# Softmax attention beside linear attention on one core: GpSimd's pattern copies as 64-bit integer additions with the addend in the instruction

## The chip, the cores and the metric

The kernel runs on one core of one Trainium2 chip. The metric is the device time of one execution in microseconds (us). It is given as the median of the runs; for the kernel before, two runs gave 650.61 and 651.38 us, with a median of 651.0 us.

## The reference, cut to what matters

Two independent attention blocks, A (linear) and B (softmax), each on 2048 tokens, model width 512, 32 heads of width 16, are computed and their outputs laid side by side:

```
# A: phi(t) = where(t > 0, t + 1, exp(t)) + 1e-6
kv  = einsum("bhsd,bhse->bhde", phi(k), v);  z = phi(k) summed over s
o   = (phi(q) @ kv) / (phi(q) . z + 1e-6)
a   = o reshaped @ wo
# B
scores = einsum("bhqd,bhkd->bhqk", q, k) * Dh ** -0.5
p      = softmax(scores, axis=-1)
b      = einsum("bhqk,bhkd->bhqd", p, v) reshaped @ wo
return concatenate([a, b], axis=-1)
```

Block B's exponentials, 32 heads of 2048 by 2048 scores, are nearly all of the work. The input is bfloat16, and so is the output.

## The kernel before, in words

**Tiling.** Block B is cut into 32 units: four groups of eight heads, four chunks of 512 queries, and two halves of each head group. A unit holds four heads, one in each 32-row quarter of TensorE, and 16 tiles of 128 keys, so 64 blocks of 128 keys by 512 queries. For each block TensorE makes the scores (line 901, into the PSUM tiles pS or pD), an engine turns them into numerators of the softmax, and TensorE multiplies these with the values (line 1284, accumulating in pPV, 17 columns a head, the last of them the sum for the denominator).

**Two ways to exponentiate.** Most blocks go through ScalarE, which writes exponentials as float16 into the tile PT (line 1113). The others go through VectorE (line 1017): it scales the score, adds a constant and converts to a 16-bit integer, and this integer's bits, read as float16, are a rough exponential. This "pattern" is called the base, version 0. Two further versions of each pattern are the same integers plus 328 and plus 656 (`SHIFT`). TensorE multiplies all three versions with values (the base with the scaled values VX, made from VV at line 714; the other two with VV) and adds them up, which evens out the error. So a block by VectorE costs TensorE three products, and somebody has to make two copies.

**Who makes the copies.** The tile DI holds 8 buffers (`NDG`), each for a group of two blocks (`DG`, 1024 patterns a partition), with room for the base and both copies. When a group's bases are there, the function `chain` hands its copies to GpSimd (`on_pool`, line 1208), or, where GpSimd has a backlog by the plan, one of the two to VectorE (`on_dve`, line 1171). `on_pool` may join neighbouring buffers: one instruction makes up to four copies (`JN`), of both versions of one or two groups, or of one version of several. It views two patterns as one int32 word and adds a word from the tile CW in which the addend stands twice; the addend is a second input, read through a broadcast view.

**What else GpSimd does.** Besides set-up at the start, it scales the values into VX (line 714, 16 times), divides each unit's result by its denominator (line 1319, 31 times, and line 1376 twice in the last unit), and does four kinds of tiny multiplications near the end for a range test (lines 680 to 699). All stand in one queue in program order.

**What sets the order.** A planner in the kernel's Python goes through all work once, with a clock for each engine and a fixed duration for each kind of step, and appends the operations to one list; this list's order is each engine's program order. The class `Sched` finds the waits: an operation waits on a semaphore of the engine whose result it reads or overwrites, and only on the operations that the keys (`reads`, `writes`) name. For GpSimd's copies the plan reserves 0.144 us (`PFX`) plus 0.833 ns for each pattern written. Block A's work and the projections are filled in between as jobs. A second program, for scores outside the range of the rough exponential, stands behind a branch at the end and isn't run with these inputs.

Of the kernel before, what the change touches and what calls it, by code (L numbers as in the profile page):

```python
# [12 lines left out]
ALU = mybir.AluOpType  # L13
# [225 lines left out]
def bass_concat_heads__linear_attn_block__softmax_full_mha__prompt_kernel(nc, A_x, A_wqkv, A_wo, B_x, B_wqkv, B_wo, out):  # L239
# [19 lines left out]
    SHIFT = (328, 656)  # L259
# [106 lines left out]
    sch = Sched()  # L366
    es = contextlib.ExitStack()
    with es:
        block = es.enter_context(nc.Block())

        def sb(name, shape, dt):
            return es.enter_context(nc.sbuf_tensor(name, shape, dt))
# [14 lines left out]
        DGW = DG * 512  # L387
        DI = sb("DI", [128, NDG * (32 + 2 * DGW + (DGW // 32) * 33 + 32)], I16)

        DIR = 32 + 2 * DGW + (DGW // 32) * 33 + 32  # L390

        def di_at(v, b):

            return b * DIR + 32 + v * DGW
        CW = sb("CW", [128, 2], mybir.dt.int32)
        DW = DI.bitcast(mybir.dt.int32)
        KR = sb("KR", [128, 2, 512], BF)
        ONL = sb("ON", [128, 12, 512], BF)
        KNa = sb("KNa", [128, NT, 256], BF)
# [121 lines left out]
        for e_ in range(2):  # L521
            sch.add("dve", lambda e, e_=e_: e.tensor_reduce(PAR[:, e_:e_ + 1], ZMk[:].rearrange("p (a e) -> p e a", e=2)[:, e_, :],
                                                           axis=AX.X, op=ALU.max),
                    reads=["ZMk"], writes=[("PAR", e_)])
# [626 lines left out]
        def chain(buf):  # L1151
# [6 lines left out]
            w = 512 * n  # L1158
# [23 lines left out]
            def on_pool(st_, en_):  # L1182
                near_ = {x[1]: x for x in pshift if x[0] == vs and x[2] == w and x[3][0] <= st_ + PMW}
                near_[buf] = me[0]
                best = [buf]
                for step in range(1, NDG):
                    run_ = [buf]
                    while (len(run_) + 1) * len(vs) <= JN and run_[-1] + step in near_:
                        run_.append(run_[-1] + step)
                    while (len(run_) + 1) * len(vs) <= JN and run_[0] - step in near_:  # L1190
                        run_.insert(0, run_[0] - step)
                    if len(run_) > len(best):
                        best = run_
                keys = []
                for b_ in best:
                    x = near_[b_]
                    pshift.remove(x)
                    if b_ != buf:
                        cands["pool"].remove(x[3])
                        st_ = max(st_, x[3][0])  # L1200
                    keys += [("DI", 0, b_, i) for i in range(n)]
                T["pool"] = en_ = st_ + PFX + len(best) * len(vs) * w * 0.000833
                gs = [(best[1] - best[0]) * DIR // 2 if len(best) > 1 else 1, len(best)]
                part = lambda t_: list(t_[:, 0:1].ap[0])
                dv = bass.AP(DW, DW[:, di_at(vs[0], best[0]) // 2:].offset, [part(DW), gs, [DGW // 2, len(vs)], [1, w // 2]])
                sv = bass.AP(DW, DW[:, di_at(0, best[0]) // 2:].offset, [part(DW), gs, [0, len(vs)], [1, w // 2]])
                cv = bass.AP(CW, CW[:, vs[0] - 1:].offset, [part(CW), [0, len(best)], [1, len(vs)], [0, w // 2]])
                sch.add("pool", lambda e: e.tensor_tensor(dv, sv, cv, op=ALU.add), reads=keys + ["CW"], writes=[("DI", v, x) for v in vs for x in best])  # L1208
                for x in best:
                    for v in vs:  # L1210
                        pv_give[x, v](en_)
            vs = (1, 2)
# [4 lines left out]
            if p_backlog(s_["t"]) - DSH * d_backlog(s_["t"]) > PSH:  # L1217
                vs = (1,)
                push("dve", s_["t"], 1, 0.06 + (w + 32) * 0.00053, on_dve)
            for v in vs:  # L1220
                pv_give[buf, v] = lambda en_, v=v: give(buf, v, "pool", en_)
            me = [(vs, buf, w, push("pool", s_["t"] + LTO["dve", "pool"], 0, PFX + len(vs) * w * 0.000833, on_pool), rk)]
            pshift.append(me[0])

# [180 lines left out]
        for t, bk, lane in ((2, SBANKS[1], "dve"), (3, SBANKS[2], "act")):  # L1405
            def tr(e, t=t, bk=bk):
# [6 lines left out]
                reads=[bk[3]], writes=[("xTb", t)])  # L1413
# [139 lines left out]
        while True:  # L1553
# [5 lines left out]
            for eng in T:  # L1559
                best = None  # L1560
                for c_ in cands[eng]:
                    st = max(pe_at("v" if isinstance(c_[3], Rounds) else "j") if eng == "pe" else T[eng], c_[0])
                    k_ = (round(st / 0.05), c_[1], c_[2])
                    if best is None or k_ < best[0]:
                        best = (k_, st, c_)
# [149 lines left out]
```

## Time and profile before

| | |
|---|---|
| median of 2 runs | 651.0 us |
| the profiled execution's own time | 651.69 us |
| its span, first to last instruction | 649.9 us |
| TensorE busy, 8355 products | 637.8 us (98%) |
| VectorE busy, 1080 instructions | 622.5 us (96%) |
| ScalarE busy, 689 instructions | 633.5 us (97%) |
| GpSimd busy, 347 instructions | 616.8 us (95%) |
| DMA, mean rate | 33 GB/s |
| mean granted TensorE clock | 0.999 |

In the profile, PE is TensorE's products, PEld its weight loads, DVE VectorE, ACT ScalarE, POOL GpSimd, and SP the engine that issues most DMAs. Busy times leave out register, branch and semaphore instructions. The profiled execution took 1.8 us more than its span, for what lies before the first and behind the last instruction. In the waits an engine's idle time is put down to what ended it. DI is the tile of the patterns, OT the tile of a unit's result, ZR its reciprocal denominators, pD and pS the scores.

### The profile page before, as it was taken

What the parts mean: (1) busy time and instruction counts of PE and PEld (TensorE: products, weight loads), DVE (VectorE), ACT (ScalarE), POOL (GpSimd) and SP (SyncE); (2) the same over time, 40 slices, a digit from 0 to 9 for tenths busy, and PEclk for the clock granted to TensorE, in tenths of its full rate; (3) what the DMA queues carried; (4) which work ended last, traced back from release to release, by engine and by line L of the source; (5) the groups of instructions that cost most, each with busy time, mean ns of one, the idle gap of its engine ahead of it and who ended that gap; (6) DMA issues with size and microseconds to landing.
All of it is one profiled execution on the core that took longest, in us unless ns stands there. A gap on an engine that the chain in (4) does not pass through costs nothing.

```text
span 649.9 us, 19218 instructions
## 1 busy us (share of the span) xinstructions
PE 637.8 (98%) x8355; PEld 214.4 (33%) x8356; DVE 622.5 (96%) x1080; ACT 633.5 (97%) x689; POOL 616.8 (95%) x347
## 2 busy tenths in 40 slices
PE   8999999999999999999999999999999999999996
PEld 5333333332333334332232323332223332223332
DVE  4999999999999999999999999999999999999974
ACT  5999999999999999999999999999999999999994
POOL 5899999999999999999999999999999999999950
PEclk9999999999999999999999999999999999999999
DMA  9701000211100110200220200011000001100212
GB/s 171 220 2 24 12 1 10 43 24 29 16 20 2 34 34 2 40 9 7 48 69 2 49 26 19 2 34 42 24 13 22 3 2 42 34 18 17 50 50 69
DMA packets 53224, 21.73 MB, mean 33 GB/s; under 512 B 44176, under 2 KB 52624, under 8 KB 53136
## 3 DMA queue, kind: packets, MB, share of 16 engines
q1 hardware_dynamic: 51664, 19.80, 13.3%
q8 instruction: 67, 1.10, 0.7%
q10 hardware_dynamic: 1472, 0.66, 0.4%
q14 instruction: 21, 0.17, 0.1%
HBM read 4.46 MB, written 4.19 MB: 13 GB/s over the span
## 4 chain that ended last, share of the span: by engine, by line
ACT 66%; PE 16%; DVE 16%; DMA 1%; issue 0%; SPq 0%
ACT PT L1113 65%; DVE DI L1017 11%; PE pPV L1284 5%; PE pS L901 5%; PE pD L611 2%; ACT EA L723 1%; PE pS L611 1%; DVE DI L1171 1%; DMA xTb<-in_B_x_dram 1%; DVE PQT L726 1%; DVE VNa L813 1%; DVE KNa L597 0%; DVE OT L1313 0%; PE pS L1336 0%; PE pD L901 0%; DMA KNa<-VNa 0%
## 5 line engine op out<-in xcount | busy, mean ns | idle before, releaser
L1113 ACT ACTIVATE PT<-pS 128x1024 f16<-128x1024 f32 (+1 forms) x651 | 619.4, 1096 | 1.9 <-PE pS L901 1.0
L1208 POOL TENSOR_TENSOR DI<-DI,CW 128x1024 int32<-128x1024 int32 (+2 forms) x264 | 580.7, 2232 | 5.8 <-DVE DI L1017 4.3
L1017 DVE TENSOR_SCALAR DI<-pD 128x512 int16<-128x512 f32 x512 | 336.9, 682 | 5.7 <-PE pD L901 3.9
L901 PE MATMUL pS<-QT,KM 32*128 32x512 bf16 x1532 | 259.5, 384 | 2.9 <-ACT PT L1113 2.0
L1284 PE MATMUL pPV<-PT,VV 128*17 128x512 f16 x1338 | 232.6, 381 | 0.0
L1284 PE MATMUL pPV<-DI,VV 128*17 128x512 f16 x1420 | 232.0, 382 | 0.1
L901 PE MATMUL pD<-QT,KM 32*128 32x512 bf16 x516 | 185.7, 384 | 0.5 <-DVE DI L1017 0.4
L1284 PE MATMUL pPV<-DI,VX 128*17 128x512 f16 x710 | 162.8, 381 | 0.4 <-DVE OT L1313 0.4
L901 PEld LDWEIGHTS pS<-QT,KM 32*128 32x128 bf16 x1532 | 65.1, 91 | 238.9 <-ACT PT L1113 190.6
L1017 DVE TENSOR_SCALAR DI<-pS 128x512 int16<-128x512 f32 x194 | 131.5, 678 | 0.3 <-PE pS L901 0.3
L1284 PEld LDWEIGHTS pPV<-PT,VV 128*17 128x17 bf16 x1338 | 52.2, 88 | 42.4 <-issue 32.4
L1284 PEld LDWEIGHTS pPV<-DI,VV 128*17 128x17 bf16 x1420 | 49.5, 88 | 45.0 <-issue 33.6
L1171 DVE TENSOR_SCALAR DI<-DI 128x1056 int16<-128x1056 int16 x73 | 49.8, 687 | 0.2
L901 PEld LDWEIGHTS pD<-QT,KM 32*128 32x128 bf16 x516 | 44.2, 91 | 7.6 <-DVE DI L1017 5.2
L1284 PEld LDWEIGHTS pPV<-DI,VX 128*17 128x17 bf16 x710 | 35.6, 88 | 21.8 <-issue 15.7
L611 PE MATMUL pD<-Wa,xTa 128*32 128x256 bf16 x640 | 26.3, 275 | 0.1
L611 PE MATMUL pD<-xTb,Wb 128*32 128x512 bf16 x288 | 23.2, 384 | 0.0
L1313 DVE STREAM_TRANSPOSE OT<-pPV 128x512 f32<-128x512 f32 x31 | 21.9, 706 | 0.0
L1319 POOL TENSOR_TENSOR OT<-OT,ZR 128x256 bf16<-128x256 f32 x31 | 19.3, 621 | 1.1 <-DVE ZR L1318 1.0
L611 PEld LDWEIGHTS pD<-Wa,xTa 128*32 128x32 bf16 x640 | 14.0, 96 | 10.3 <-issue 6.1
L597 DVE CAST KNa<-pD 128x512 bf16<-128x512 f32 x21 | 14.3, 681 | 3.1 <-PE pD L611 3.1
L714 POOL TENSOR_SCALAR VX<-VV 128x544 bf16<-128x544 bf16 x16 | 10.2, 646 | 6.5 <-DVE VV L711 6.5
(139 smaller groups left out, 381.5 us busy)
## 6 DMA issues: line engine op xcount, KB each, us to landing
out_dram<-KNa SPq DMA_DIRECT2D x31, 128.0 KB, 1.7
Wa<-in_A_wqkv_dram SPq DMA_DIRECT2D x1, 1536.0 KB, 8.0
KM<-KR SPq DMA_DIRECT2D x96, 16.0 KB, 1.8
Wb<-in_B_wqkv_dram SPq DMA_DIRECT2D x2, 384.0 KB, 5.7
Wb<-in_B_wqkv_dram SPq DMA_DIRECT2D x1, 512.0 KB, 4.7
Wa<-in_A_wo_dram SPq DMA_DIRECT2D x1, 512.0 KB, 4.3
Wa<-in_B_wo_dram SPq DMA_DIRECT2D x1, 512.0 KB, 3.8
ON<-in_B_x_dram ACTq DMA_DIRECT2D x1, 256.0 KB, 2.9
```

The source lines that it names most:

```text
L597: return lambda e, bk: (e.tensor_copy(out_fn(), in_fn(bk)) if lane == "dve" else e.activation(out_fn(), in_fn(bk), ACTF.Copy))
L611: ins = self.e.matmul(out_[32 * g:32 * g + 32], lhsT=lhsT[:, 32 * g:32 * g + 32], rhs=rhs, start=start, stop=stop, tile_position=(0, 32 * g))
L714: st.append(("pool", 0.61, f_op("pool", lambda e: e.tensor_scalar(VX[:, r, 4 * t4:4 * t4 + 4, :].rearrange("p t c -> p (t c)"), VV[:, r, 4 ...
L723: ("act", 0.0635 + n * 0.000833, f_ev("act", lambda e, bk: e.activation(EA[:, 0:n], f32v(bk)[:, c0:c0 + n], ACTF.Exp), [], ["EA"])),
L901: return e.matmul(dst, lhsT=KM[32 * g:32 * g + 32, Gp % 2, e_, j * 128:(j + 1) * 128], rhs=QT[32 * g:32 * g + 32, Gp % 2, c * 512:(c + 1) ...
L1017: sch.add("dve", lambda e: e.tensor_scalar(DI[:, di_at(0, buf) + i * 512:di_at(0, buf) + (i + n) * 512], f32v(DBANK[b0], n * 512), ESC, EB ...
L1113: sch.add("act", lambda e: e.activation(PTf[:, p0 * 512:p0 * 512 + w], S5[:, c0:c0 + w], ACTF.Exp, scale=SC), reads=skeys(sl, len(bl)), wr ...
L1171: sch.add("dve", lambda e: e.tensor_scalar(gapped(DI, di_at(2, buf), wide // 32, 32), DI[:, di_at(0, buf) - 32:di_at(0, buf) + w], 1.0, fl ...
L1208: sch.add("pool", lambda e: e.tensor_tensor(dv, sv, cv, op=ALU.add), reads=keys + ["CW"], writes=[("DI", v, x) for v in vs for x in best])
L1284: sch.add("pe", lambda e, g=g, j=j, c0=c0, V_=V_, r2=r2, P=P, first=first, last_=last_: e.matmul(PVb[32 * g:32 * g + 17, 0:512] if len(P.s ...
L1313: sch.add("dve", lambda e: e.transpose(OT[:, 0, :], PVb[:, 0:512]), reads=[("PV", g) for g in range(4)], writes=[("OT", 0)])
L1319: ("pool", 0.59, f_op("pool", lambda e: e.tensor_tensor(xn[:, :, 16 * e_:16 * e_ + 16], o[:, :, 0:16], zr.unsqueeze(2).broadcast_to([128, ...
```

## The change: what it does

The int32 addition of `on_pool` is replaced by GpSimd's addition of 64-bit integers, `int64_add`. One word now holds four patterns, and the addend, 328 or 656 four times, stands in the instruction, so that nothing is read but the base. An instruction makes one version only; where one instruction made both, two now follow each other, version 1 first. Groups that were joined stay joined. The planner's clock and its fixed durations are not touched, and the order of every other engine's program is what it was.

```diff
-        DW = DI.bitcast(mybir.dt.int32)
+        DW = DI.bitcast(mybir.dt.uint64)
...
                 T["pool"] = en_ = st_ + PFX + len(best) * len(vs) * w * 0.000833
-                gs = [(best[1] - best[0]) * DIR // 2 if len(best) > 1 else 1, len(best)]
-                part = lambda t_: list(t_[:, 0:1].ap[0])
-                dv = bass.AP(DW, DW[:, di_at(vs[0], best[0]) // 2:].offset, [part(DW), gs, [DGW // 2, len(vs)], [1, w // 2]])
-                sv = bass.AP(DW, DW[:, di_at(0, best[0]) // 2:].offset, [part(DW), gs, [0, len(vs)], [1, w // 2]])
-                cv = bass.AP(CW, CW[:, vs[0] - 1:].offset, [part(CW), [0, len(best)], [1, len(vs)], [0, w // 2]])
-                sch.add("pool", lambda e: e.tensor_tensor(dv, sv, cv, op=ALU.add), reads=keys + ["CW"], writes=[("DI", v, x) for v in vs for x in best])
+                at64 = lambda v: bass.AP(DW, DW[:, di_at(v, best[0]) // 4:].offset, [list(DW[:, 0:1].ap[0])] +
+                                         ([[(best[1] - best[0]) * DIR // 4, len(best)]] if len(best) > 1 else []) + [[1, w // 4]])
+                for v in vs:
+                    word = int.from_bytes(struct.pack("<4H", *[SHIFT[v - 1]] * 4), "little")
+                    sch.add("pool", lambda e, v=v, word=word: e.int64_add(at64(v), at64(0), word), reads=keys, writes=[("DI", v, x) for x in best])
```

In the built program the 264 instructions of line 1208 become 465 of line 1207: 297 over 512 32-bit words of a partition (256 64-bit words) and 168 over 1024 (512 64-bit words). The lines behind move up by one. The rows below are GpSimd's program around the result of the second unit, before:

```order
L1208 TENSOR_TENSOR DI<-DI,CW 128x2x1024 [waits s_dve] x2
L1208 TENSOR_TENSOR DI<-DI,CW 128x512
L1319 TENSOR_TENSOR OT<-OT,ZR 128x16x16 [waits s_dve]
L1208 TENSOR_TENSOR DI<-DI,CW 128x2x1024
L1208 TENSOR_TENSOR DI<-DI,CW 128x512 [waits s_dve]
```

and the same place in the changed program, where line 1207 is the copies and line 1318 the division:

```order
L1207 ISA DI<-DI 128x2x512 [waits s_dve]
L1207 ISA DI<-DI 128x2x512
L1207 ISA DI<-DI 128x512
L1318 ISA
L1318 TENSOR_TENSOR OT<-OT,ZR 128x16x16 [waits s_dve]
L1207 ISA
L1207 ISA DI<-DI 128x2x512 x2
L1207 ISA DI<-DI 128x512 [waits s_dve]
```

Each joined copy is two instructions now, and on either side of the division stands a row without operands or a wait (`L1318 ISA`, `L1207 ISA`) that the program before does not have. The same happens around the values VX, here the third and fourth of them, before:

```order
L1208 TENSOR_TENSOR DI<-DI,CW 128x1024 [waits s_dve]
L714 TENSOR_SCALAR VX<-VV 128x544 [waits s_dve]
L1208 TENSOR_TENSOR DI<-DI,CW 128x1024 [waits s_dve] x2
```

and changed:

```order
L1207 ISA
L1207 ISA DI<-DI 128x512 [waits s_dve]
L1207 ISA DI<-DI 128x512
L714 ISA
L714 TENSOR_SCALAR VX<-VV 128x544 [waits s_dve]
L1207 ISA
L1207 ISA DI<-DI 128x512 [waits s_dve]
L1207 ISA DI<-DI 128x512
```

These bare rows stand wherever the kind of work on GpSimd changes between the 64-bit addition and the other instructions: 43 ahead of a run of copies, and 43 ahead of other work (31 at line 1318, 11 at line 714, 1 at line 680). The program before has one such row among its work, at line 494 in the set-up, which the changed program has as well. On the other engines nothing moved; TensorE's products with the copies wait on GpSimd's semaphore for each version apart.

## The prediction

> **What bounds the kernel now.** I read the summary of the page first, then the chain that ended last, GpSimd's groups by form, the waits, and the timeline at two places. In the first two:
>
> ```profile
> PE 637.8 (98%) x8355; PEld 214.4 (33%) x8356; DVE 622.5 (96%) x1080; ACT 633.5 (97%) x689; POOL 616.8 (95%) x347
> ...
> ACT 66%; PE 16%; DVE 16%; DMA 1%; issue 0%; SPq 0%
> ...
> L1208 POOL TENSOR_TENSOR DI<-DI,CW 128x1024 int32<-128x1024 int32 (+2 forms) x264 | 580.7, 2232 | 5.8 <-DVE DI L1017 4.3
> ```
>
> All four engines are nearly full, but the chain runs through ScalarE, TensorE and VectorE, and GpSimd has no share in it. It is just fast enough. The waits say the same, and how near it is:
>
> ```profile
> PEld pS L901 <- ACT PT L1113: 190.6, 472, 0.9
> ...
> PEld pPV L1284 <- POOL DI L1208: 5.0, 20, 0.4
> ...
> POOL DI L1208 <- DVE DI L1017: 4.3, 6, 1.4
> ```
>
> TensorE waits for ScalarE to empty score banks all the time, and for GpSimd's copies only 20 times, 5.0 us in all. So making GpSimd's copies faster can win about 5 us, and a GpSimd that stands still reaches TensorE soon, because TensorE's program is in a fixed order and everything behind a product that lacks its copy waits with it: the next scores, and through them ScalarE and VectorE.
>
> **The change, part 1: the copies themselves.** By form:
>
> ```profile
> L1208 POOL TENSOR_TENSOR DI<-DI,CW 128x2048 int32<-128x2048 int32 x79 | 283.4, 3600 | 1.7 <-DVE DI L1017 0.5
> L1208 POOL TENSOR_TENSOR DI<-DI,CW 128x1024 int32<-128x1024 int32 x132 | 246.9, 1892 | 4.1 <-DVE DI L1017 3.8
> L1208 POOL TENSOR_TENSOR DI<-DI,CW 128x512 int32<-128x512 int32 x53 | 55.0, 1039 | 0.0
> L1319 POOL TENSOR_TENSOR OT<-OT,ZR 128x256 bf16<-128x256 f32 x31 | 19.3, 621 | 1.1 <-DVE ZR L1318 1.0
> L714 POOL TENSOR_SCALAR VX<-VV 128x544 bf16<-128x544 bf16 x16 | 10.2, 646 | 6.5 <-DVE VV L711 6.5
> ...
> L1376 POOL TENSOR_TENSOR OT<-OT,ZR 128x128 bf16<-128x128 f32 x2 | 0.8, 402 | 2.4 <-DVE ZR L1375 2.4
> L680 POOL TENSOR_TENSOR GRW<-GRW,ZMk 128x32 f32<-128x32 f32 x2 | 0.5, 252 | 4.4 <-DVE GRW L678 4.4
> ```
>
> The three forms of L1208 add up to 585.3 us, 580.7 on the page, where overlaps count once. From 512 to 1024 words a copy grows by 853 ns, from 1024 to 2048 by 1708: 1.67 ns a word on some 186 ns that every instruction pays. The trace has no 64-bit addition. From below: a 64-bit word costs what a 32-bit word costs with one input, by the row of L714 at most 646 / 544 = 1.19 ns. From above: it costs two 32-bit words, 3.33 ns. I take 1.67 ns, one element of an addition, since the second input, which a 32-bit word had as well, is gone. Then the 297 small instructions (256 words) cost 186 + 427 = 613 ns and the 168 large ones (512 words) 1041 ns: 182 + 175 = 357 us, where 581 us stood. That is 224 us less work on GpSimd, in spite of 201 instructions more. On its own this gains next to nothing, as shown: the time is set elsewhere.
>
> **Part 2: the bare rows.** There are 86, 43 ahead of copies and 43 ahead of other work, at each change of kind. [...]
>
> ```profile
> 0.80 0.20 POOL L493 MEMSET identb<- 128x128 bf16 x1 [0.29 <-POOLq L1700]
> 1.24 0.29 POOL L494 TENSOR_SCALAR_AFFINE_SELECT identb<-identb 128x128 bf16<-128x128 bf16 x1 [0.24 <-POOL identb L493]
> ```
>
> [...]
>
> ```profile
> Wa<-in_A_wqkv_dram SPq DMA_DIRECT2D x1, 1536.0 KB, 8.0
> KM<-KR SPq DMA_DIRECT2D x96, 16.0 KB, 1.8
> ...
> Wb<-in_B_wqkv_dram SPq DMA_DIRECT2D x1, 512.0 KB, 4.7
> ```
>
> A short transfer takes 1.8 us from issue to landing, a middling load 4.7, the largest 8.0. I take one load and one short transfer to start and end it, 4.7 + 1.8 = 6.5, and about 0.3 for the dispatch (0.24 above): 6.8 us, an estimate from these rows; the range goes from 4.7 to 8.0. Nothing else on GpSimd can run meanwhile. The rows have no wait of their own, so an exchange begins as soon as the work ahead of it is done and can overlap the wait of the instruction behind it.
>
> [...]
>
> **Part 3: what a round costs.** GpSimd leaves its copies for other work and comes back 42 times (31 + 11; the 43rd return never comes), each time after two exchanges, 13.6 us, and the other work itself. The cover is what TensorE can do before it needs the first copy made after the return. At the second unit's end:
>
> ```profile
> 49.52 8.34 POOL L1208 TENSOR_TENSOR DI<-DI,CW 128x2048 int32<-128x2048 int32 x3
> 51.90 1.28 DVE L1017 TENSOR_SCALAR DI<-pD 128x512 int16<-128x512 f32 x2
> ...
> 57.81 0.62 POOL L1319 TENSOR_TENSOR OT<-OT,ZR 128x256 bf16<-128x256 f32 x1
> ...
> 58.40 8.15 POOL L1208 TENSOR_TENSOR DI<-DI,CW 128x2048 int32<-128x2048 int32 x3
> ...
> 62.12 0.09 PEld L1284 LDWEIGHTS pPV<-DI,VV 128*17 128x17 bf16 x1 [0.23 <-POOL DI L1208]
> ```
>
> VectorE has the bases at 53.2; two large additions and a small one end at 53.2 + 2.1 + 0.6 = 55.9, 1.9 us sooner than now. TensorE asks at 62.1. Less the division (0.62) and the first new copy (1.04), the cover is 62.1 - 55.9 - 1.7 = 4.5 us, and TensorE stands still for 13.6 - 4.5 = 9.1. Near the end of the program:
>
> ```profile
> 598.58 1.28 DVE L1017 TENSOR_SCALAR DI<-pD 128x512 int16<-128x512 f32 x2
> ...
> 603.73 0.62 POOL L1319 TENSOR_TENSOR OT<-OT,ZR 128x256 bf16<-128x256 f32 x1
> ...
> 608.87 0.09 PEld L1284 LDWEIGHTS pPV<-DI,VV 128*17 128x17 bf16 x2 [0.23 <-issue]
> ```
>
> Bases at 599.9, two small copies to 601.1, TensorE asks at 608.9: cover 608.9 - 601.1 - 0.62 - 0.61 = 6.6 us, stall 7.0. Read in this way, the rounds have covers between 2.7 and 8.1 us, 5.0 in the mean. 42 rounds x (13.6 - 5.0) = 361 us. Some rounds follow so soon that the cover is already spent:
>
> ```profile
> 172.20 0.62 POOL L1319 TENSOR_TENSOR OT<-OT,ZR 128x256 bf16<-128x256 f32 x1
> 172.78 1.89 POOL L1208 TENSOR_TENSOR DI<-DI,CW 128x1024 int32<-128x1024 int32 x1
> 174.64 0.64 POOL L714 TENSOR_SCALAR VX<-VV 128x544 bf16<-128x544 bf16 x1
> 175.30 1.89 POOL L1208 TENSOR_TENSOR DI<-DI,CW 128x1024 int32<-128x1024 int32 x1
> 177.16 0.65 POOL L714 TENSOR_SCALAR VX<-VV 128x544 bf16<-128x544 bf16 x1
> ```
>
> Seven rounds begin within 4.5 us of the one before, two of them here; at some 4 us each that is 28 more. Elsewhere the faster copies catch up between rounds, since they need six tenths of the old time. The exchange ahead of the first copies and the one at line 680 hide behind waits but for a few us, which I leave out.
>
> **The sum**, against the profiled execution's own 651.7 us (0.1% above the median, 651.0): 651.7 + 361 + 28 = 1041, say **1040 us**. A second way gives a floor. GpSimd has to do 357 us of copies, 30 of other work behind the first two VX (19.3 + 14 x 0.646 + 0.8 + 0.5 and a little) and 86 x 6.8 = 585 of exchanges, one after the other: 972. What lies before and behind shows in the first row below, the second VX, and in the last, GpSimd's last instruction:
>
> ```profile
> 14.98 0.65 POOL L714 TENSOR_SCALAR VX<-VV 128x544 bf16<-128x544 bf16 x1 [0.69 <-DVE VV L711]
> ...
> 642.04 0.40 POOL L1376 TENSOR_TENSOR OT<-OT,ZR 128x128 bf16<-128x128 f32 x1 [0.15 <-DVE ZR L1375]
> ```
>
> 15.6 us ahead, 649.9 - 642.4 = 7.5 behind, and 1.8 outside the span, so the floor is 997 us. So GpSimd becomes the engine that sets the end, with only some 45 us in which it waits.
>
> With 4.7 us a row the sum by covers is 651.7 + 42 x (9.4 - 5.0) + 28 = 865 (floor 816), with 8.0 it is 651.7 + 42 x (16.0 - 5.0) + 28 = 1142.
>
> **Rivals.** *The rows cost nothing*: if all code stays in place, 86 x 0.24 = 21 us are added to GpSimd and 224 taken away. GpSimd then is idle a third of the time, no round exceeds its cover, and the kernel loses its 5.0 us of waits for copies: 651.7 - 5.0 = 647 us, within 2%. [...] 5%.
>
> *A short exchange*: at 1.8 us, the shortest landing, a round is 3.6 us and lies below the mean cover of 5.0; a few rounds with a cover of 3 lose under 1 us, and close ones some 3 each: 651.7 + 7 x 3 - 5 = 668 at most, 647 where the waits for copies pay for it. The point from which it decides is half of the mean cover, 2.5 us a row. I put its time at 655. 4%.
>
> *The addition is slow*: if a 64-bit word costs two 32-bit ones, 297 x 1.04 + 168 x 1.89 = 626 us of copies, and GpSimd's own sum is 626 + 30 + 585 + 25 = 1266 us. Then GpSimd never catches up and is the only bound. For it: a carry from half to half must be made. Against: the addend is no longer read. 7%.
>
> *GpSimd's freed time speeds up VectorE*, whose instructions may stop losing time to GpSimd's transfers, by more than 2%, with cheap rows. VectorE's share of the chain is 16%, so I see little room. 1%.
>
> **How the numbers follow.** The forecast, exchanges between 4.7 and 8.0 us, has 83%. Rows that cost nothing or little have 9%, the slow addition 7%, a gain 1%. The range 870 to 1190 us is the forecast's bounds, a little wider at the top for a longer exchange; what is outside is the cheap rows and the slow addition, under 2 in 10. Slower by over 2%, about what a measurement of this kernel can tell from no change: 0.90; within 2%: 0.09; faster: 0.01.
>
> **What would show it.** GpSimd's busy time falls from 617 to about 390 us, since an exchange is idle time in such a profile: ahead of each division, each VX and each run of copies there are 5 to 8 us without work, 86 times, and the 64-bit additions take about 0.61 and 1.04 us. TensorE's waits for GpSimd's copies rise from 5.0 us to several hundred, in 40 or so pieces of 5 to 10 us. ScalarE's and VectorE's busy times stay, so their shares fall to about 60%. The prediction is wrong if those gaps are missing (then the time is near 650), if they are there and TensorE's waits are not (then the covers are longer than I read), or if the additions take over 1.5 us.

## The result and the profile after

The changed kernel takes 1112.3 us in the median of two runs (1109.99 and 1114.61), where 651.0 us stood: a ratio of 1.709, with a 95% interval from 1.693 to 1.725. The forecast was 1040 us, in a range from 870 to 1190. The profiled execution has a span of 1112.8 us and a mean granted TensorE clock of 0.786; before, these were 649.9 us and 0.999. Of the runs below, the profiled execution of e4 was slow as a whole (723.8 us, where its four others took 705.5 to 707.2), so its span is not used.

From the page of the profile after: the busy times, the chain that ended last, GpSimd's additions and division, and TensorE's products with the patterns (busy time and mean in ns, then the idle time before them and what ended most of it).

```profile
PE 763.2 (69%) x8355; PEld 224.7 (20%) x8356; DVE 639.8 (57%) x1080; ACT 652.0 (59%) x689; POOL 386.8 (35%) x548
...
PE 34%; issue 32%; DVE 24%; POOL 7%; ACT 4%; DMA 0%; DVEq 0%; POOLq 0%
...
L1207 POOL INT64_ADD DI<-DI x465 | 348.1, 760 | 392.6 <-issue 219.7
L1283 PE MATMUL pPV<-DI,VV 128*17 128x512 f16 x1420 | 279.0, 439 | 274.9 <-POOL DI L1207 270.7
```

Four nearly full engines have become four half idle ones. GpSimd has lost 230 us of work and is the emptiest of all, and yet TensorE stands 270.7 us ahead of products that want its copies. "issue" in the chain is time in which an engine waits for nothing that the profile shows. It holds 32% of the chain, 0% before.

The waits, as engine, what it was about to do, whom it waited for, and then the us in total, the times and the longest:

```profile
PEld pPV L1283 <- POOL DI L1207: 307.9, 86, 15.3
PE pPV L1283 <- POOL DI L1207: 270.7, 52, 15.0
...
POOL DI L1207 <- issue: 219.7, 37, 6.7
DVE DI L1017 <- PE pD L901: 214.3, 108, 12.7
...
POOL DI L1207 <- DVE DI L1017: 147.7, 99, 6.5
...
POOL OT L1318 <- issue: 134.3, 19, 7.6
...
POOL VX L714 <- issue: 73.1, 10, 8.6
...
DVE ON L1323 <- POOL OT L1318: 69.1, 12, 16.0
```

The weight loads' 307.9 us and the products' 270.7 us are largely the same time, seen on two queues. On GpSimd, 37 gaps of 219.7 / 37 = 5.9 us stand ahead of copies, 19 of 7.1 ahead of divisions and 10 of 7.3 ahead of VX, and nothing that the profile shows ends them. What stands at their place in GpSimd's queue is in the views of lines 1207 and 1318 (durations as minimum, median and maximum in ns):

```profile
L1207 POOL INT64_ADD DI<-DI x465: 601/611/1042, 22.7 to 1084.5; - x155
L1207 POOLq MODIFY_POOL_CONFIG  x86: 1/1/11, 15.3 to 1074.5; - x86
...
L1318 POOLq MODIFY_POOL_CONFIG  x62: 1/11/12, 69.5 to 1066.5; - x62
```

The bare rows have a name now. Each leaves two records: 86 for the 43 rows at line 1207, 62 for the 31 at line 1318, and likewise at lines 714 and 680. A record takes 1 to 12 ns. The price of a row is the gap behind it. Such a row with its gap is what the prediction calls an exchange; what GpSimd does in the gap no run shows. VectorE's and GpSimd's timelines at the third unit's end (start, duration, in brackets the idle time ahead and what ended it):

```profile
67.85 0.23 DVE L1317 RECIPROCAL ZR<-OT 128x16 f32<-128x16 f32 x1
...
67.42 2.05 POOL L1207 INT64_ADD DI<-DI  x2 [2.34 <-DVE DI L1017]
76.59 0.61 POOL L1318 TENSOR_TENSOR OT<-OT,ZR 128x256 bf16<-128x256 f32 x1 [7.12 <-DVE DI L1017]
83.04 3.65 POOL L1207 INT64_ADD DI<-DI  x4 [5.84 <-issue]
```

The copies end at 69.47. The division comes 7.12 us later, though ZR, which VectorE makes for it, was ready at 67.85 + 0.23 = 68.08 (the base that the row names is not the division's; it only was VectorE's last result before it). The next copies come 5.84 us after the division. For one division of 0.61 us GpSimd is away for 13.6 us. What the other engines do meanwhile shows in a table by stages of 5 us (busy us and instructions of PE, PEld, DVE, ACT and POOL, then the granted clock):

```profile
70.00:75.00 5.00, 4.42 (x77) 1.58 (x73) 4.84 (x9) 5.00 (x7) 0.00 (x0) 1.00 0.02 5
75.00:80.00 5.00, 0.00 (x0) 0.00 (x0) 0.91 (x2) 0.36 (x1) 0.61 (x1) 0.75 0.00 0
80.00:85.00 5.00, 0.88 (x7) 0.20 (x7) 0.00 (x0) 0.00 (x0) 1.96 (x2) 0.50 0.00 0
85.00:90.00 5.00, 5.00 (x66) 1.61 (x63) 3.56 (x6) 3.65 (x4) 3.74 (x5) 0.72 0.00 0
90.00:95.00 5.00, 4.62 (x67) 1.61 (x64) 4.88 (x9) 5.00 (x7) 1.98 (x2) 1.00 0.02 3
```

For 5 us TensorE has work left; then it, VectorE and ScalarE all stop, as the prediction said. The last column but two says something that it did not say. The clock falls to 0.75 in the stage in which TensorE stands, to 0.50 in the next, and is full again only in the fifth. Here 66 products need 5.00 us, where 77 took 4.42 before the stop. The last two columns, the share and the GB/s of the DMA, show no transfer from 75 to 85 us, and the whole gap ahead of the copies, 77.2 to 83.0, lies in that stretch.

**Where the 463 us are.** TensorE's two numbers in the first row, with the span, divide the whole difference. It is idle for 1112.8 - 763.2 = 349.6 us, where it was idle for 649.9 - 637.8 = 12.1: 337.5 us more. And the same 8355 products keep it busy for 763.2 us in place of 637.8: 125.4 us more. The two add up to 462.9, the difference of the spans.

### The profile page after: what moved, and what is told of

It is laid out like the page before. It is cut to its first block, busy times and chain, and to the rows that moved or that the text cites. A ratio compares the mean times of both kernels' runs of the same rounds, so it can differ in the third digit from the quotient of the medians.

```text
span 1112.8 us, 19591 instructions
## 1 busy us (share of the span) xinstructions
PE 763.2 (69%) x8355; PEld 224.7 (20%) x8356; DVE 639.8 (57%) x1080; ACT 652.0 (59%) x689; POOL 386.8 (35%) x548
## 2 busy tenths in 40 slices
DMA packets 53227, 21.75 MB, mean 20 GB/s; under 512 B 44176, under 2 KB 52624, under 8 KB 53136
## 4 chain that ended last, share of the span: by engine, by line
PE 34%; issue 32%; DVE 24%; POOL 7%; ACT 4%; DMA 0%; DVEq 0%; POOLq 0%
DVE DI L1017 16%; PE pPV L1283 13%; PE pS L901 11%; PE pD L611 4%; POOL DI L1207 4%; ACT PT L1113 3%; PE pS L611 2%; POOL OT L1318 2%; DVE DI L1171 1%; PE pD L901 1%; DVE KNa L597 1%; DVE EC L724 1%; POOL VX L714 1%; DVE OT L1312 1%; DVE VV L711 1%
## 5 line engine op out<-in xcount | busy, mean ns | idle before, releaser
L1113 ACT ACTIVATE PT<-pS 128x1024 f16<-128x1024 f32 (+1 forms) x651 | 636.7, 1070 | 446.4 <-PE pD L901 248.8
L1017 DVE TENSOR_SCALAR DI<-pD 128x512 int16<-128x512 f32 x512 | 341.5, 684 | 267.6 <-PE pD L901 214.3
L1207 POOL INT64_ADD DI<-DI x465 | 348.1, 760 | 392.6 <-issue 219.7
L1283 PE MATMUL pPV<-DI,VV 128*17 128x512 f16 x1420 | 279.0, 439 | 274.9 <-POOL DI L1207 270.7
L901 PE MATMUL pS<-QT,KM 32*128 32x512 bf16 x1532 | 292.6, 435 | 7.7 <-DVE DI L1017 5.3
L1283 PE MATMUL pPV<-PT,VV 128*17 128x512 f16 x1338 | 275.2, 431 | 0.0
L901 PE MATMUL pD<-QT,KM 32*128 32x512 bf16 x516 | 211.7, 440 | 37.8 <-DVE DI L1017 31.4
L1283 PE MATMUL pPV<-DI,VX 128*17 128x512 f16 x710 | 189.1, 429 | 0.3 <-DVE OT L1312 0.2
L1283 PEld LDWEIGHTS pPV<-DI,VV 128*17 128x17 bf16 x1420 | 53.1, 90 | 358.8 <-POOL DI L1207 307.9
L1318 POOL TENSOR_TENSOR OT<-OT,ZR 128x256 bf16<-128x256 f32 x31 | 18.9, 610 | 220.9 <-issue 134.3
L1323 DVE STREAM_TRANSPOSE ON<-OT 128x512 bf16<-128x512 bf16 x12 | 8.5, 711 | 69.1 <-POOL OT L1318 69.1
L714 POOL TENSOR_SCALAR VX<-VV 128x544 bf16<-128x544 bf16 x16 | 10.2, 640 | 85.0 <-issue 73.1
L611 PE MATMUL pD<-Wa,xTa 128*32 128x256 bf16 x640 | 31.7, 310 | 9.1 <-DVE KR L649 4.6
L611 PE MATMUL pS<-Wa,xTa 128*32 128x256 bf16 x384 | 20.4, 325 | 0.0
```

The source lines that it names most:

```text
L611: ins = self.e.matmul(out_[32 * g:32 * g + 32], lhsT=lhsT[:, 32 * g:32 * g + 32], rhs=rhs, start=start, stop=stop, tile_position=(0, 32 * g))
L714: st.append(("pool", 0.61, f_op("pool", lambda e: e.tensor_scalar(VX[:, r, 4 * t4:4 * t4 + 4, :].rearrange("p t c -> p (t c)"), VV[:, r, 4 ...
L901: return e.matmul(dst, lhsT=KM[32 * g:32 * g + 32, Gp % 2, e_, j * 128:(j + 1) * 128], rhs=QT[32 * g:32 * g + 32, Gp % 2, c * 512:(c + 1) ...
L1017: sch.add("dve", lambda e: e.tensor_scalar(DI[:, di_at(0, buf) + i * 512:di_at(0, buf) + (i + n) * 512], f32v(DBANK[b0], n * 512), ESC, EB ...
L1113: sch.add("act", lambda e: e.activation(PTf[:, p0 * 512:p0 * 512 + w], S5[:, c0:c0 + w], ACTF.Exp, scale=SC), reads=skeys(sl, len(bl)), wr ...
L1207: sch.add("pool", lambda e, v=v, word=word: e.int64_add(at64(v), at64(0), word), reads=keys, writes=[("DI", v, x) for x in best])
```

## The experiments

Three questions were open. Is it the exchange, and not the addition, that costs the time? What are the copies worth without it? And what are the 125 us of longer products, and the stalls beyond the forecast's, made of? No kernel here leaves work out. e2 adds tiny additions on scratch data, and e5 and e9 add products with zero weights, which add nothing to the sums; all others do the kernel's own work, on other engines or in another order.

### Without the returns: e1_no_return, e4_moved_only and e3_vx_rounds

e1 is the changed kernel with all that GpSimd does between copies given to VectorE, at the same places in the order. One exchange is left at the start and one at the end.

```diff
-            st.append(("pool", 0.61, f_op("pool", lambda e: e.tensor_scalar(
+            st.append(("pool", 0.61, f_op("dve", lambda e: e.tensor_scalar(
...
-                  ("pool", 0.59, f_op("pool", lambda e: e.tensor_tensor(xn[:, :, 16 * e_:16 * e_ + 16], o[:, :, 0:16],
+                  ("pool", 0.59, f_op("dve", lambda e: e.tensor_tensor(xn[:, :, 16 * e_:16 * e_ + 16], o[:, :, 0:16],
```

> The changed kernel with the 31 divisions and the 16 scalings of VX on VectorE at the same places of the order, so that GpSimd has only the 64-bit additions between set-up and the end: one exchange at the start, one at the end, no round. Theory (the rounds are the whole cost): about 655 us; 651.7, less up to 5 of waits for copies, plus what VectorE takes on, 31 x 0.35 + 16 x 0.2 = 14 us, of which part shows; between 645 and 670. Rival (the 64-bit additions or their 201 extra instructions and semaphores cost something themselves): over 700.

e4 is its control: the same two lines changed in the kernel before, with the int32 copies.

> The kernel before with its int32 copies and only the divisions and scalings of VX moved to VectorE, as the control for the first run. Theory: 650 to 670 us, GpSimd loses 29 us of work and VectorE gains some 14. The difference between the first run and this one is what the 64-bit addition is worth by itself: by the 5.0 us of waits, at most 5 us. Rival: the first run is over 10 us faster than this one, so that GpSimd's speed mattered more than the waits said.

e3 gives only the division away (the second pair of lines) and keeps VX on GpSimd, so 11 rounds of two exchanges are left.

> The changed kernel with only the divisions moved to VectorE, so that 11 of the 42 rounds are left, those of VX. Theory: each round costs what it does in the changed kernel, (1112 - 651) / 42 = 11.0 us, so 655 + 11 x 11.0 = 776; if close rounds are dearer, up to 800. Rival (a fixed cost, or the additions): near 1112 or near 660, not in proportion to the rounds.

**Measured.** e1 took 673.1 us (ratio 1.034, 1.032 to 1.035), 3 us above the expected range, with the 64-bit additions all in place. So the additions are not what costs 461 us, and the rival of the slow addition is dead twice over (a median of 611 ns, and this). Of the 22 us that e1 takes over the kernel before, VectorE's added work is the likely cause, not a shown one: division and VX take VectorE 22.4 us there, and VectorE holds 75% of the chain. e3, measured once like e2 below, took 800.3 us, at the upper end of what was expected (776, up to 800 where close rounds are dearer). A round costs (800.3 - 673.1) / 11 = 11.6 us there; all 42 cost (1112.3 - 673.1) / 42 = 10.5 each. The time goes up with the number of rounds.

e4 missed. It took 705.9 us (ratio 1.085, 1.083 to 1.086), so the 64-bit copies are worth 33 us in this place, where the theory said 5 at most; its rival was right. VectorE's rows by form show why. In e1 they are

```profile
L1318 DVE TENSOR_TENSOR OT<-OT,ZR 128x256 bf16<-128x256 f32 x31 | 17.6, 569 | 0.0
...
L714 DVE TENSOR_SCALAR VX<-VV 128x544 bf16<-128x544 bf16 x16 | 4.8, 300 | 0.1
```

and in e4

```profile
L1319 DVE TENSOR_TENSOR OT<-OT,ZR 128x256 bf16<-128x256 f32 x31 | 46.6, 1503 | 0.0
...
L714 DVE TENSOR_SCALAR VX<-VV 128x544 bf16<-128x544 bf16 x16 | 9.9, 619 | 0.1
```

The same division on the same data takes VectorE 569 ns in the mean in e1 and 1503 in e4. The difference of both rows is 29.0 + 5.1 = 34 us of VectorE's time, the size of the 33. Line 1017, which reads from PSUM, takes 680 ns in e4 and 679 in e1, so not all of VectorE's work is slower. Single divisions say where the time goes, first two of e1 and e4 with the GpSimd additions that ran when they began, and then all 31 of each (minimum, median, maximum in ns):

```profile
197.41 2.05 POOL L1207 INT64_ADD DI<-DI  x2 [1.99 <-DVE DI L1017]
198.54 1.20 DVE L1318 TENSOR_TENSOR OT<-OT,ZR 128x256 bf16<-128x256 f32 x1
...
608.54 7.32 POOL L1208 TENSOR_TENSOR DI<-DI,CW 128x2048 int32<-128x2048 int32 x2
612.70 3.44 DVE L1319 TENSOR_TENSOR OT<-OT,ZR 128x256 bf16<-128x256 f32 x1
...
L1318 DVE TENSOR_TENSOR OT<-OT,ZR x31: 406/415/1195, 42.2 to 636.7; 128x256 bf16<-128x256 f32 x31
L1319 DVE TENSOR_TENSOR OT<-OT,ZR x31: 405/1141/3842, 42.7 to 693.9; 128x256 bf16<-128x256 f32 x31
```

In both cases the division ends 0.28 us after the addition does: at 199.74 behind 199.46, at 616.14 behind 615.86. The shortest of the 31 take 406 and 405 ns. So in these two the time hangs on how long GpSimd's instruction still runs. Those of e4 last 1.0 to 3.6 us, those of e1 0.6 to 1.04, and GpSimd is busy for 594 us in e4 and 362 in e1. The scaling of VX, with one input in SBUF, does the same: 1.60 to 1.62 us behind additions of 1.89 us, at most 0.35 us behind those of 0.61. That the additions of e4 read two inputs and those of e1 one need not be the cause; no run holds their length fixed. Why the division and the scaling take longer there and line 1017 does not, no run shows either.

### The exchange without the addition: e2_exchange_only

The kernel before, with its int32 copies. At each of the 42 returns one 64-bit addition of four words on a scratch tile, which nobody waits for, is put ahead of the first copy. So GpSimd has two exchanges a round, as after the change, while all real work stays as it was.

```diff
+                if away[0] and away[1]:
+                    sch.add("pool", lambda e: e.int64_add(TW64[:, 1, :], TW64[:, 0, :], 1), reads=["TW"], writes=["TW1"])
+                away[:] = [False, True]
                 sch.add("pool", lambda e: e.tensor_tensor(dv, sv, cv, op=ALU.add), ...
```

> The kernel before with its int32 copies as they were, and one 64-bit addition of 4 words on a scratch tile behind each of the 42 visits to other work, ahead of the next copy, so that every visit costs two exchanges and nothing else is new. Theory: the copies are slower than in the changed kernel (581 us against 348) and the rounds the same, so GpSimd's own sum is 581 + 30 + 42 x 13.0 + 25 = 1182 us, and the time 1182 to 1330. Rival (the cost lies in the additions on the copies): about 660.

**Measured:** 1223.5 us, within the 1182 to 1330 that were expected. From its waits, where TW is the scratch tile and line 1221 the int32 copies:

```profile
PE pPV L1297 <- POOL DI L1221: 472.1, 49, 13.5
...
POOL DI L1221 <- issue: 297.9, 42, 7.8
POOL TW L1219 <- issue: 247.7, 42, 6.7
```

The exchange to the 64-bit addition takes 247.7 / 42 = 5.9 us, the one back to ordinary arithmetic 297.9 / 42 = 7.1, together 13.0 a round, the same as after the change. It is shown that the exchange by itself, with the copies as they were, costs more than the change did: 572 us over the kernel before, against 461 with the 64-bit copies. The difference of 111 us is what their saving is worth once GpSimd has exchanges to catch up with.

### The clock: e5_fill and e9_fill_more

Are the 125 us of longer products the slow clock after the stalls, and what do they cost? In e5 TensorE gets 2099 products with zero weights in the stalls, ahead of the first product that needs a copy made after a return, each stall's number cut to its length in the trace.

```diff
+            def pre(e, n_=n_, g=o.pv):
+                for i in range(n_):
+                    e.matmul(PVb[32 * g:32 * g + 17, 0:256], lhsT=ZW[:, 0:17], rhs=Wb[:, 0, 1024:1280], start=False, stop=False, tile_position=(0, 32 * g))
+            o.pre = pre
```

> The changed kernel, with products of zero weights on TensorE ahead of the first product that waits for a copy after each return: as many (0 to 130 of 0.107 us) as fill most of the stall there in the changed kernel, some 225 us in all, all the other work as it was. Theory (after every stall TensorE runs at half clock for some 4 us and more, and this is the excess over the forecast): the granted clock rises from 0.79 to over 0.9, the waits of GpSimd for VectorE's bases fall, and the time falls from 1112 towards 1040, 1030 to 1075. Rival (the excess comes from the stalls themselves, one behind the division on VectorE and one behind the copies, whatever the clock): within 10 us of 1112, or longer by products that come too late.

e9 adds 749 more in the stalls that e5 left open, 16 of them where TensorE stands behind VectorE's wait for a division.

> The changed kernel with products of zero weights on TensorE in the stalls, as in the run with the fill, and now also in 16 stalls that were left there, of 2.9 to 7.2 us, in which TensorE waits for VectorE while that waits for the division of a finished unit (57 us in all), and somewhat more in 11 of the others. Theory (half clock after stalls is what is left to gain): the granted clock rises from 0.92 to 0.96 or more, and the time falls from 1078 to 1045 to 1065. Rival (what is over the forecast there is the second stall itself, not the clock): 1070 to 1080.

**Measured:** e5 took 1078.3 us (1076.1 to 1080.3; ratio 1.656, 1.651 to 1.660) at a clock of 0.917, just above the upper edge of what the theory of the clock gave it. e9 took 1072.6 us (1070.3 to 1074.8; ratio 1.647, 1.643 to 1.650) at 0.97. For the last step the rival's range held: with the clock nearly full, 40 us in all are back. The same window as above, in e5:

```profile
75.00:80.00 5.00, 5.00 (x49) 4.21 (x47) 1.27 (x3) 0.72 (x1) 0.61 (x1) 1.00 0.02 3
80.00:85.00 5.00, 3.62 (x34) 2.82 (x31) 0.00 (x0) 0.00 (x0) 0.98 (x1) 1.00 0.00 0
85.00:90.00 5.00, 4.89 (x81) 1.69 (x82) 3.93 (x7) 4.12 (x5) 4.70 (x6) 1.00 0.01 3
```

VectorE and ScalarE stand still as before, but the clock stays at 1.00, and behind the stall 81 products go through in a stage where 66 did. Why so little of the 125 comes back is seen when the added products are taken out of TensorE's busy time. From the pages of e5 and e9 the first rows:

```profile
PE 940.9 (87%) x10455; PEld 415.9 (39%) x10455; DVE 635.0 (59%) x1080; ACT 645.4 (60%) x689; POOL 386.4 (36%) x548
...
PE 988.6 (92%) x11204; PEld 476.8 (45%) x11204; DVE 632.4 (59%) x1080; ACT 645.3 (60%) x689; POOL 386.4 (36%) x548
```

and from TensorE's groups by form the added products, first e5's, then the two kinds of e9:

```profile
L1647 PE MATMUL pPV<-Wb,ZW 128*17 128x256 bf16 x2099 | 250.0, 282 | 0.0
...
L1649 PE MATMUL pPV<-Wb,ZW 128*17 128x256 bf16 x2099 | 236.9, 274 | 0.0
...
L1660 PE MATMUL pPV<-Wb,ZW 128*17 128x256 bf16 x749 | 87.3, 275 | 0.0
```

In e5 the real products take 940.9 - 250.0 = 690.9 us, 72 less than after the change. But the time in which TensorE does no real work, idle or filled, is 1076.5 - 690.9 = 385.6 us, 36 more than 349.6. A TensorE that is fast again comes sooner to the product whose copy is missing, and waits there longer: about half of what the slow clock takes had lain beside the exchange. (Some of the 36 us may be added products that ran on after the copy was there.) In e9 the real products take 988.6 - 324.2 = 664.4 us, 99 less, and the time without real work is 1070.8 - 664.4 = 406.4 us, 57 more.

The last step is not a clean one. The products of line 1649 mostly end before the copy is there: behind 31 of their 41 stretches TensorE still waits. Those of line 1660 in part hold up real work. One stretch runs from 222.0 to 226.0 us ahead of two score products, which stood ahead of the stall before, and ScalarE waits 3.96 us for them. So 40 us is what the runs show the clock to be worth at least; the whole of its price is open.

### A second stall: e10_late_transpose

VectorE's transpose of a finished pair of units waits for GpSimd's second division, 69.1 us in 12 places by the waits above, and bases queue behind it. The theory is that VectorE's bases and emptied score banks come late behind this wait, and that the part of the excess that the clock does not explain comes from it. In e10 the transpose of the first three head groups stands about ten VectorE instructions later; the list `held` keeps it back until then. Nothing else moves on any engine.

```diff
-                st.append(("dve", 0.626, f_op("dve", lambda e: e.transpose(on_at(k), XN[:, xb, :]), [("XN", xb, 0), ("XN", xb, 1)], on_keys(k))))
+                st.append(("dve", 0.626, (lambda bk: sch.held.append((len(sch.lane_ops["dve"]) + 12, on_keys(k), [("XN", xb, 0), ("XN", xb, 1)], lambda: sch.add(
+                    "dve", lambda e: e.transpose(on_at(k), XN[:, xb, :]), reads=[("XN", xb, 0), ("XN", xb, 1)], writes=on_keys(k)))))
+                          if Gp < NGP - 1 else ...
```

> [...] Then the time falls from 1112 to between 1050 and 1090 us, VectorE's wait for the division falls from 82 us to under 25, and GpSimd's wait for bases from 148 us to about 100. Rival: the wait lies beside the exchange back to the 64-bit addition that follows each division (5.9 us), and beside TensorE's own stall, so that nothing hangs on it: the time stays within 10 us of 1112, and VectorE's wait moves to other places.

**Measured:** 1122.8 us (1120.0 to 1123.5; ratio 1.723, 1.719 to 1.727), 10.5 us slower: far from the theory's 1050 to 1090, and just outside the rival's 10 us. In its waits, where line 1212 is the copies, no wait of the 12 moved transposes is left, but

```profile
PE pPV L1288 <- POOL DI L1212: 333.5, 52, 14.8
DVE DI L1022 <- PE pD L906: 257.1, 121, 12.5
...
POOL DI L1212 <- DVE DI L1022: 142.8, 100, 4.4
```

TensorE's wait for copies has grown from 270.7 to 333.5 us, and VectorE's for scores from 214.3 to 257.1. GpSimd's wait for bases is what it was, 143 in place of 148. So of the theory's three signs only the shorter wait for the division came (14.0 us are left), and the rival was right in its main point: nothing is gained when that wait goes, since others grow in its place. Why the time rose by 10 us instead of staying is open.

### Is the 64-bit addition of use without the exchange? e6, e7 and e8

e6 is e1 with the 73 copies that the plan gives to VectorE (line 1171) made by GpSimd as well, since it is now idle nearly half of the time.

```diff
-                sch.add("dve", lambda e: e.tensor_scalar(gapped(DI, di_at(2, buf), wide // 32, 32), DI[:, di_at(0, buf) - 32:di_at(0, buf) + w], 1.0, float(SHIFT[1]),
-                                                         op0=ALU.mult, op1=ALU.add), reads=rk, writes=[("DI", 2, buf)])
+                sch.add("pool", lambda e: e.int64_add(at64(2), at64(0), word), reads=rk, writes=[("DI", 2, buf)])
```

> The kernel of the first run (64-bit additions, no round, divisions and VX on VectorE) with the 73 copies that VectorE made (line 1171) made by GpSimd too, by 64-bit additions at the same places of the order. Theory (in the first run VectorE became the bound, 75% of the chain, since it took on 22 us): VectorE's work falls by 50 us, the chain goes back to ScalarE, and the time to 645 to 655, as the kernel before. Rival (GpSimd's copies come later there than VectorE's did, or 64-bit additions hinder VectorE): 665 or more.

e7 divides the work as e1 does, but tells the planner what the new copies and the moved work cost, and its table of weights was searched anew for that plan.

```diff
-    PFX = 0.144
+    PFX = 0.186
...
-                T["pool"] = en_ = st_ + PFX + len(best) * len(vs) * w * 0.000833
+                T["pool"] = en_ = st_ + len(vs) * (PFX + len(best) * w * 0.000417)
...
-            st.append(("pool", 0.61, f_op("pool", lambda e: e.tensor_scalar(
+            st.append(("dve", 0.27, f_op("dve", lambda e: e.tensor_scalar(
```

> The same division of work (64-bit additions without a round, divisions and VX on VectorE, every copy on GpSimd), with the planner told of it (186 ns and 0.417 ns a pattern for each addition, 0.5 us for a division, 0.27 for VX) and its parameters by stretch of time chosen anew, so that the order is a new one. ScalarE's work is the same, 629 us by the plan. Theory: ScalarE stays the bound and the time is 645 to 655; a gain over the kernel before of at most 1%. Rival (the order of before was fitted to its waits and a new one loses some): 655 to 670.

e8 is e7 with GpSimd's last ordinary work, the range test (lines 678 and 695 to 697 there) and the last unit's division, on VectorE.

> The kernel of the run before this (a new order, 64-bit additions for every copy) with the last ordinary work of GpSimd, the multiplications of the range test and the last unit's division, on VectorE too, at the same places. There the new order had put the range test between the copies, at 527, 543 and 559 us, so that it had three rounds. Theory (a round costs 10 to 13 us): 691 less 3 x 11.5 = 656, 650 to 662. Rival (the new order is slow for another reason): above 675.

**Measured.** e6: 665.0 us (ratio 1.022, 1.021 to 1.024), 10 us above the theory's range, where the rival's begins (665 or more). VectorE's busy time fell from 640.1 to 607.0 us for only 8 us of time, so VectorE was not alone in setting the end of e1. e7: 691.1 us (1.061, 1.060 to 1.063), a miss of both theories. GpSimd's timeline near its end shows what the new order had done:

```profile
526.70 0.24 POOL L678 TENSOR_TENSOR GRW<-GRW,ZMk 128x32 f32<-128x32 f32 x1 [7.00 <-issue]
533.00 3.54 POOL L1205 INT64_ADD DI<-DI  x6 [6.05 <-DVE VNa L811]
543.50 0.24 POOL L678 TENSOR_TENSOR GRW<-GRW,ZMk 128x32 f32<-128x32 f32 x1 [6.96 <-issue]
549.51 2.37 POOL L1205 INT64_ADD DI<-DI  x4 [5.76 <-issue]
558.86 0.18 POOL L695 TENSOR_TENSOR TP<-TP 1x1 f32<-1x1 f32 x1 [6.99 <-DVE DI L1015]
...
565.49 7.23 POOL L1205 INT64_ADD DI<-DI  x12 [5.92 <-issue]
```

The range test, which stood behind most copies before, stood among them now: three rounds, each for under 1 us of work. e8 takes these away (and the exchange ahead of the last unit's division) and needs 662.7 us (1.017, 1.016 to 1.019), 28.4 less and 0.7 above the theory's range. It has a new exchange, though, in GpSimd's set-up, as the row of e7 and that of e8 show:

```profile
1.48 0.29 POOL L492 TENSOR_SCALAR_AFFINE_SELECT identb<-identb 128x128 bf16<-128x128 bf16 x1 [0.49 <-POOL identb L491]
...
10.31 0.28 POOL L492 TENSOR_SCALAR_AFFINE_SELECT identb<-identb 128x128 bf16<-128x128 bf16 x1 [9.32 <-issue]
```

This is the bare row that the kernel before has too, and that idles for 0.2 to 0.5 us in every other run. e8 is the only kernel whose last work on GpSimd is a 64-bit addition. Whether that is the cause is not shown: it is one profile, and no run tries it by itself. ScalarE's instructions, which are the same in both, start 6.7 us later in e8 than in e7 from there up to the range test, and 25.5 us earlier behind it. So the three rounds cost 32.2 us, 10.7 each: three strays cost 5%. No version came below the kernel before: 662.7 and 665.0 against 651. Of e8's last 11 us some 7 are this exchange; what holds the rest was not settled. In e8's chain TensorE has 69%.

## Why the prediction was right, point by point

**The bare rows (part 2): right.** They were read as exchanges at 6.8 us each. Measured are 5.9 ahead of copies; ahead of other work GpSimd's groups by form after the change have, behind the bar, the idle time and what ended it:

```profile
L1318 POOL TENSOR_TENSOR OT<-OT,ZR 128x256 bf16<-128x256 f32 x31 | 18.9, 610 | 220.9 <-issue 134.3 <-DVE DI L1017 65.0 <-DVE EC L724 14.5
L714 POOL TENSOR_SCALAR VX<-VV 128x544 bf16<-128x544 bf16 x16 | 10.2, 640 | 85.0 <-issue 73.1 <-DVE DI L1017 7.2 <-DVE VV L711 4.7
...
L680 POOL TENSOR_TENSOR GRW<-GRW,ZMk 128x32 f32<-128x32 f32 x2 | 0.5, 246 | 11.4 <-issue 7.8 <-DVE GRW L678 3.6
```

That is 220.9 / 31 = 7.1 us a division, 73.1 + 7.2 = 80.3 for the 11 VX behind copies, and 7.8 once. With 43 x 5.94 + 1.4 for a longer first one the exchanges come to 566 us, 6.6 a row. What carried the forecast was the place of the rows in the program's order. That the price came so near is luck in good part: it was the author's estimate, put together from loads of other data (4.7 + 1.8 + 0.3), and no run shows this term; what the runs showed in its place are the gaps of 5.9 and 7.1 us. Nor does a run show that a transfer is what takes the time. The profile has 53227 DMA packets after and 53224 before, and the windows above show no transfer in the gap ahead of the copies.

**The additions (part 1): right.** 613 and 1041 ns were forecast; the trace has a median of 611 and a longest of 1042, in all 348.1 us for 357. "On its own this gains next to nothing" held as far as it could be tried: with no round left (e1, e6, e8) nothing was gained. But e1 against e4 shows a gain that the forecast gave a chance of 1%: VectorE's division and VX take 34 us less there. In the kernel before both are on GpSimd.

**The stalls (part 3): right in kind, near in size.** The forecast had 361 + 28 = 389 us of stalls; TensorE is idle 337.5 us longer. With the measured 13.0 us a round the forecast's own rule gives 42 x (13.0 - 5.0) + 28 = 364, and with the clock kept up (e9) TensorE is without real work for 406.4 - 12.1 = 394. That answers to a cover of 4.3 us in place of 5.0 (42 x (13.0 - 4.3) + 28 = 393), worked out and not shown by itself; what e9's second fill held up is in it.

**What was mis-sized: the sum had no term for TensorE's clock.** It took every product outside the stalls at the speed of before, where the clock was 0.999 in the mean, and where the trace shows half clock only in its last 1.4 us. In the stall shown above TensorE stops at about 74.4 us, and 0.75 over 75 to 80 us means half clock from 77.5, 3.1 us later; it resumes at about 84.1, and 0.72 over 85 to 90 us means half clock until about 87.8, for 3.7 us of work. In all the products take 125.4 us longer. The trace of before shows the fall once, at its end: the last product (start, duration), and two stages of 1 us.

```profile
644.72 0.38 PE L1336 MATMUL pS<-Wa,xTb 128*128 128x512 bf16 x1
...
648.00:649.00 1.00, 0.00 (x0) 0.00 (x0) 0.00 (x0) 0.00 (x0) 0.00 (x0) 0.76 0.12 29
649.00:650.00 1.00, 0.00 (x0) 0.00 (x0) 0.00 (x0) 0.00 (x0) 0.00 (x0) 0.50 0.03 8
```

The product ends at 645.1 us, and 0.76 over 648 to 649 us means half clock from 648.5, 3.4 us later. This stood beside a forecast of 42 stalls of about 9 us, and should have been in it. The price of the slow clock, by e5 and e9, is 40 us or more; by e5 about half of the longer products lies in the cover. The forecast with the measured exchange is 651.7 + 364 = 1016; e9 lies 57 above this, 27 of it what is left of longer products (664.4 - 637.8) and 30 the shorter cover with what the second fill held up, and 40 more lead on to 1112. The sum is right to 72 us in part because two errors point opposite ways: the exchange was put 0.6 us a round too dear, and clock and cover were put too cheap.

**The floor (997 us, "some 45 us in which it waits"): the rule is right, the wait failed.** GpSimd's own sum with the measured numbers is 348 + 29 + 566 + 25 = 968 us, and it waits 147.7 for bases. The loop from its copies through TensorE and VectorE back to it was slower than forecast; e9 brings that wait down to 117.0 with the time.

**The rivals.** That the rows cost nothing, or that the exchange is short, is refuted by e2; that the addition is slow, by its row. (The shortest landing on the page before is 1.7 us, not 1.8; it changes nothing.) The signs named ahead came: GpSimd's busy time 386.8 (about 390 forecast), gaps of 5.8 to 8.6 us at the 86 rows, shares of 57 and 59% for VectorE and ScalarE, 52 waits of TensorE of 5 us in the mean. Only the busy times of VectorE and ScalarE did not quite stay; they rose by 17 and 19 us.

## What to carry to other kernels

Look at what stands between an engine's instructions, and not only at the instructions: 64-bit additions (a median of 0.61 us) and divisions (0.61 us) are each cheap on GpSimd here, and the two exchanges of a round cost 13.0 us at every return, so either one kind goes to another engine wholly or the work is gathered into few runs. Here even that only brought the time back to within 2% of the kernel before. When a stall is forecast on TensorE, price the slow clock behind it too (half clock for 3.7 us behind the stall shown, 125.4 us of longer products in all), and take off what of that lies in the next cover (about half in e5). And try the remedy with its control: moving the division and VX looked like a loss of 55 us in one version and of 22 in the other, and what differed beside them was how long GpSimd's additions ran (up to 3.6 us against 1.04; GpSimd busy for 594 us against 362).

## What the runs showed of the hardware that was not expected

- The exchange is not the same both ways: 5.9 us to the 64-bit addition, 7.1 back to ordinary arithmetic, in the changed kernel, in e2 and in e7 alike. In the changed kernel a gap of 5.8 to 8.6 us stands at each of the 86 changes of kind, and not only at the first. In e8 the first ordinary work behind such a row in the set-up comes after 9.3 idle us as well.
- A 64-bit addition with the addend in the instruction takes as long a word as an int32 addition of two tensors: (1042 - 611) / 256 = 1.68 ns after, where 853 / 512 = 1.67 stood before, so twice as many patterns in the same time.
- In the two cases shown, a VectorE division of 256 elements a partition that began while a GpSimd addition ran ended 0.28 us after that addition, which had one input in e1 and two in e4. The shortest divisions take 0.41 us, the longest 3.8 us, in e4, where the additions last up to 3.6 us in the mean of a form. The scaling of 544 elements took 1.60 to 1.62 us behind additions of 1.89 us, and at most 0.35 us behind those of 0.61.
- The half clock of TensorE cost less than the products lost: in e5 72 us of longer products came back, and 36 us of the span.
